# A linear-attention layer with a fused feed-forward network: two-input work moved off GpSimd, wider weight conversion, mask by copy and select, gather by chunk, first block by parts

## The chip, the cores and the metric

The kernel runs on one core of one Trainium2 chip. The metric is the device time of one execution in microseconds, taken as the median of several executions. The core has five engines with instruction queues of their own: TensorE (PE in the profile; its weight loads are PEld), VectorE (DVE), ScalarE (ACT), GpSimd (POOL) and SyncE (SP). SP only issues DMAs here.

## The reference

```python
def _attn_ref(q, k, v, f_logit):            # (4, 8, 768, 48) each
    f = 1.0 / (1.0 + np.exp(-f_logit))
    for t in range(S):
        state = f[:, :, t, :, None] * state + np.einsum('bhd,bhe->bhde', k[:, :, t], v[:, :, t])
        y[:, :, t] = np.einsum('bhd,bhde->bhe', q[:, :, t], state)
    return y

def _moe_ref(x, w1, w2, w3, w_out):         # x (3072, 384), w1, w2 (384, 1024)
    a = x @ w1
    b = x @ w2
    h = a * b @ w3                          # w3 (1024, 1024)
    return h @ w_out                        # w_out (1024, 384)

x = attn_out.transpose(0, 2, 1, 3).reshape(3072, 384)
```

The four weight matrices arrive as 64-bit floats. The kernel gets them as pairs of 32-bit words (low, high) and has to make 32-bit floats of them on the chip.

## The kernel before

**Attention.** The 3072 tokens are 24 chunks of 128 (`u`, six to each of four sequences). For a chunk, ScalarE makes the gates (`gates`), VectorE runs a product scan forward (`forward`, tile fwd) and one backward from the inverse of the chunk's last product (`ends`, `backward`, tile bwd), and scales q and k by them (Q, K). TensorE makes all pairs Q by K (`pairs`, two tiles pa), VectorE masks them with the tile `causal` (`mask`, tile A, two instructions of 128x512), and TensorE makes the outputs py from A and v and from the previous state (`value`). K is turned by TensorE (pk), copied by ScalarE (kt) and multiplied by v (pd); VectorE updates the state S with it (`state`), and GpSimd copies it into block form (`blocks`, tile sb). `outcome` on ScalarE copies py to ys.

**Feed-forward network.** It runs over 8 blocks of three chunks. `gather` moves a block's ys into the layout xt by ten DMAs, once all three chunks are there. `up` computes x@w1 and x@w2 in 16 groups of three products of 384 columns (L421; the trace shows each 32-bit product as two matmuls). `keep_a` copies the one on ScalarE, `times` multiplies on VectorE (tile ab). Since nothing non-linear follows, w3@w_out is folded once into wc: eight folds of eight products (`fold`, L573), each copied by VectorE (`folded`). `down` multiplies ab by wc, three groups of eight products a block (L456), and needs all eight folds.

**Weight conversion.** `fetch` loads a piece of 512 columns (384 for w_out) of word pairs and makes floats of it in six passes: two on ScalarE (`magnitude` L504, `rest` L508), a clamp on GpSimd (L511), a shift (L515) and a sign pass (L519) on VectorE, and an integer addition of two tiles on GpSimd (`joined`, L522). There are 36 pieces: 12 of w1 and w2, 8 of w_out, 16 of w3.

**Order.** Every step is a task of `Plan` with an engine, an estimated cost, what it depends on and a priority. `Plan.order` places the tasks one after the other in an imagined timetable, and the instructions are emitted in that order. Each engine then works through its list strictly in order, so an instruction that waits holds up everything behind it on its engine. `need(u)` is the time by which a chunk is wanted, used as a priority. A flag tells at the end whether the ranged form was accurate; if not, a general form runs. The flag is loaded on each engine after all its other work.

Of the kernel before, what the change touches and what calls it, by code (L numbers as in the profile page):

```python
# [31 lines left out]
U32 = mybir.dt.uint32  # L32
ALU = mybir.AluOpType
# [4 lines left out]
P = 128  # L38
# [14 lines left out]
NW = 512  # L53
NAB = 21
LOW = float.fromhex("0x1p-15")
HIGH = float.fromhex("0x1.dffffep+16")
# [58 lines left out]
def kernel(  # L115
# [16 lines left out]
    w1s = const.tile([P, KM, DFF], F32, name="w1s")  # L132
    w2s = const.tile([P, KM, DFF], F32, name="w2s")
    wc = const.tile([P, KF, DM], F32, name="wc")
    left = const.tile([1, 1], I32, name="left")
    with tc.manual_schedule():
        ranged(tc, q, k, f_logit, v, w1, w2, w3, w_out, out, ident, w1s, w2s, wc, left)
        outside = nc.values_load(left[0:1, 0:1], min_val=0, max_val=1)
        with tc.If(outside > 0, preferred_fallthrough_block=False):
            general(tc, q, k, f_logit, v, leaf_mask, out, ident, w1s, w2s, wc)  # L140
# [7 lines left out]
def ranged(ctx, tc, q, k, f_logit, v, w1, w2, w3, w_out, out, ident, w1s, w2s, wc, left):  # L148
# [5 lines left out]
    loads = ctx.enter_context(tc.tile_pool(name="loads", bufs=4))  # L154
    work = ctx.enter_context(tc.tile_pool(name="work", bufs=2))
    work3 = ctx.enter_context(tc.tile_pool(name="work3", bufs=3))
    raws = ctx.enter_context(tc.tile_pool(name="raws", bufs=4))
    wos = ctx.enter_context(tc.tile_pool(name="wos", bufs=KF))
# [5 lines left out]
    causal = keep.tile([P, C], F32, name="causal")  # L164
    first = keep.tile([R, NQ], F32, name="first")
    back = keep.tile([R, NQ], F32, name="back")
    gate = [keep.tile([R, NQ + 1], F32, name=f"gate{i}") for i in range(2)]
    lead = [keep.tile([R, HP], F32, name=f"lead{i}") for i in range(4)]
    qs, ks, fs = ([keep.tile([R, NQ], F32, name=f"{nm}{i}") for i in range(n)] for nm, n in (("q", 3), ("k", 3), ("f", 2)))
    sb = [keep.tile([R, HP, R], F32, name=f"sb{i}") for i in range(2)]  # L170
    least = keep.tile([R, HP], F32, name="least")
    ysum = keep.tile([R, NU], F32, name="ysum")
    ones = keep.tile([R, 1], F32, name="ones")

# [6 lines left out]
    def setup():  # L181
        for t in fs:
            nc.gpsimd.memset(t[32:64], 30.0)
        for t in qs + ks:
            nc.gpsimd.memset(t[32:64], 0.0)
        nc.vector.memset(first, 0.0)
        nc.vector.memset(heads(first)[:, :, 0], 1.0)
        for t in [back] + gate:
            nc.vector.memset(t, 0.0)
        nc.vector.memset(least, 1.0)  # L190
        nc.vector.memset(ones, 1.0)
        make_identity(nc, ident)
        nc.gpsimd.memset(causal, 1.0)
        nc.gpsimd.affine_select(
            out=causal, in_=causal, pattern=[[1, C]], compare_op=ALU.is_ge, fill=0.0, base=0,
            channel_multiplier=-1,
        )
        for t in sb:
            nc.gpsimd.memset(t, 0.0)
# [5 lines left out]
    def need(u):  # L205
        return 9.0 * u if u < UB else 45.0 + 17.0 * (u - UB)
# [4 lines left out]
    def attention(u):  # L211
        s, t = st[u], tk[u]
        b = u // NCH
# [9 lines left out]
        t["lf"] = plan.add("SP", 0.75, load(fs[u % 2], f_logit), past(u, 2, "g"), n0 - 30, lag=2.2)  # L223
        t["lq"] = plan.add("SP", 0.75, load(qs[u % 3], q), past(u, 3, "q"), n0 - 29, lag=2.2)
        t["lk"] = plan.add("SP", 0.75, load(ks[u % 3], k), past(u, 3, "k"), n0 - 28, lag=2.2)
# [5 lines left out]
        t["lv"] = plan.add("SP", 0.75, load_v, past(u, 4, "v", "s"), n0 - 27, lag=2.2)  # L231

        def gates():
            g, f = gate[u % 2], heads(fs[u % 2])
            nc.scalar.activation(heads(g[:, 0:NQ])[:, :, 1:C], f[:, :, 1:C], AF.Sigmoid)  # L235
            nc.scalar.activation(lead[u % 4], f[:, :, 0], AF.Sigmoid)

        t["g"] = plan.add("ACT", 0.85, gates, [t["lf"]] + past(u, 2, "r") + past(u, 5, "d"), n0)
# [3 lines left out]
        def forward():  # L242
            s["P"] = one.tile([R, NQ], F32, name="fwd")
            nc.vector.tensor_tensor_scan(  # L244
                s["P"], gate[u % 2][:, 0:NQ], first, 0.0, ALU.mult, ALU.add
            )

        t["p"] = plan.add("DVE", 1.1, forward, [t["g"]] + past(u, 1, "q", "i"), n0)
# [705 lines left out]
```

## Time and profile before

| | |
|---|---|
| runs | 585.24, 588.34, 589.01 us; median 588.34 |
| profiled execution | 584.74 us, span 583.0 us |
| mean granted TensorE clock | 0.967 |
| busy: PE / DVE / ACT / POOL | 524.1 / 248.7 / 127.6 / 118.3 us |

A row of the timeline has start, duration, engine, line, operation, written tile <- read tiles, shape and count; in brackets stands the idle time before it and what ended that. A row of groups has the count, then busy time in us and mean duration in ns, then idle time before. A row of the windows view has the window, then for PE, PEld, DVE, ACT and POOL the busy time and count, the granted clock, and the DMA share and rate.

### The profile page before, as it was taken

How to read it: one execution, taken by the hardware profiler on the slowest of the kernel's cores; microseconds unless marked ns; L12 is line 12 of the kernel's file. 1: busy time of each engine (PE TensorE's matmuls, PEld its weight loads, DVE VectorE, ACT ScalarE, POOL GpSimd, SP SyncE). 2: the span in 40 equal slices, each digit the busy share in tenths (PEclk: the TensorE clock that was granted, in tenths of full speed). 3: DMA queues.
4: the chain of work that ended last, by engine and by line, in shares of the span. 5: the costliest groups of instructions: out<-in, count | busy, mean ns of one | idle time of the engine just before them, and what ended most of it. 6: DMA issues, size and time to landing. Idle time of an engine off the chain costs nothing.

```text
span 583.0 us, 7033 instructions
## 1 busy us (share of the span) xinstructions
PE 524.1 (90%) x2610; PEld 331.3 (57%) x2610; DVE 248.7 (43%) x450; ACT 127.6 (22%) x277; POOL 118.3 (20%) x130
## 2 busy tenths in 40 slices
PE   2633996989999999989998999899999999999994
PEld 2522654656777666556655755565555555555552
DVE  7898997799999572118311611001101101100100
ACT  2552652432332221012111111111101101101100
POOL 3698885880222020000000100000000000000000
PEclk9966897999999999999999999999999999999998
DMA  6754757654534340022001100100010020000000
GB/s 191 237 185 144 246 197 228 187 167 129 172 116 134 104 136 28 1 68 82 15 0 51 32 15 0 55 28 0 15 54 15 0 67 15 0 13 28 0 15 32
DMA packets 25706, 46.68 MB, mean 80 GB/s; under 512 B 4928, under 2 KB 14144, under 8 KB 25664
## 3 DMA queue, kind: packets, MB, share of 16 engines
q1 hardware_dynamic: 25664, 46.16, 26.0%
q8 instruction: 22, 0.36, 0.3%
q14 instruction: 20, 0.16, 0.1%
HBM read 36.70 MB, written 4.72 MB: 71 GB/s over the span
## 4 chain that ended last, share of the span: by engine, by line
PE 61%; DVE 4%; SPq 3%; DMA 1%; issue 1%; ACT 0%; ACTq 0%; DVEq 0%
PE f L421 36%; PE f L456 19%; SPq L402 3%; PE py L328 2%; PE py L334 2%; PE pa L287 1%; DMA xt<-ys 1%; DVE bwd L270 1%; DVE A L298 1%; PE pd L350 1%; DVE fwd L244 1%; PE pk L310 1%; ACT ys L380 0%; DMA vt<-in_v_dram 0%; DVE Q L264 0%
## 5 line engine op out<-in xcount | busy, mean ns | idle before, releaser
L421 PE MATMUL f<-xt,w1s 128*128 128x384 f32 x384 | 136.4, 492 | 0.5 <-DVE ab L436 0.5
L421 PE MATMUL f<-xt,w2s 128*128 128x384 f32 x384 | 134.9, 488 | 0.0
L436 DVE TENSOR_TENSOR ab<-f,a 128x384 f32<-128x384 f32 x64 | 35.5, 555 | 227.1 <-PE f L421 227.1
L456 PE MATMUL f<-wc,ab 128*128 128x384 f32 x384 | 126.7, 487 | 0.0
L421 PEld LDWEIGHTS f<-xt,w1s 128*128 128x128 f32 x384 | 73.2, 192 | 50.6 <-DVE ab L436 1.1
L456 PEld LDWEIGHTS f<-wc,ab 128*128 128x128 f32 x384 | 72.2, 190 | 48.7
L421 PEld LDWEIGHTS f<-xt,w2s 128*128 128x128 f32 x384 | 72.2, 190 | 48.5
L430 ACT COPY a<-f 128x384 f32<-128x384 f32 x64 | 30.6, 477 | 193.0 <-PE f L421 193.0
L287 PE MATMUL pa<-Q,K 48*128 48x128 f32 x384 | 32.5, 316 | 41.6 <-DVE K L278 41.4
L371 POOL COPY sb<-S 48x192 f32<-48x192 f32 x40 | 25.0, 625 | 185.8 <-PE py L334 123.2
L287 PEld LDWEIGHTS pa<-Q,K 48*128 48x128 f32 x384 | 27.5, 216 | 48.2 <-issue 33.2
L298 DVE TENSOR_TENSOR A<-pa,causal 128x512 f32<-128x512 f32 x48 | 30.7, 679 | 30.6 <-PE py L328 25.0
L573 PE MATMUL f<-wo,w3s 128*128 128x384 f32 x128 | 43.2, 494 | 0.0
L328 PE MATMUL py<-A,vt 128*48 128x128 f32 (+1 forms) x384 | 29.8, 296 | 5.9 <-ACT ys L380 5.2
L573 PEld LDWEIGHTS f<-wo,w3s 128*128 128x128 f32 x128 | 24.4, 194 | 16.2 <-issue 0.6
L504 ACT ACTIVATE magnitude<-raw 128x512 f32<-128x512 f32 (+1 forms) x36 | 23.5, 653 | 40.8 <-POOL w3s L522 21.0
L511 POOL TENSOR_SCALAR magnitude<-magnitude 128x512 f32<-128x512 f32 (+1 forms) x36 | 29.5, 826 | 14.3 <-ACT magnitude L504 14.1
L328 PEld LDWEIGHTS py<-A,vt 128*48 128x48 f32 (+1 forms) x384 | 23.3, 140 | 15.9 <-issue 7.1
L244 DVE TENSOR_TENSOR_SCAN fwd<-gate,first 112x512 f32<-112x512 f32 x24 | 31.0, 1292 | 3.0 <-ACT gate L235 2.9
L515 DVE TENSOR_SCALAR magnitude<-magnitude 128x512 uint32<-128x512 uint32 (+1 forms) x36 | 27.6, 770 | 7.1 <-POOL magnitude L511 7.1
L465 ACT COPY o<-f 128x384 f32<-128x384 f32 x24 | 11.4, 477 | 86.7 <-PE f L456 86.7
L519 DVE SCALAR_TENSOR_TENSOR rest<-raw,rest 128x512 uint32<-128x512 uint32 (+1 forms) x36 | 28.5, 801 | 3.9 <-DMA k<-in_k_dram 2.1
(56 smaller groups left out, 347.2 us busy)
## 6 DMA issues: line engine op xcount, KB each, us to landing
raw<-in_w_dram SPq DMA_DIRECT2D x28, 512.0 KB, 4.4
f<-in_f_logit_dram SPq DMA_DIRECT2D x48, 96.0 KB, 2.8
q<-in_q_dram SPq DMA_DIRECT2D x48, 96.0 KB, 2.5
k<-in_k_dram SPq DMA_DIRECT2D x48, 96.0 KB, 2.5
vt<-in_v_dram SPq DMA_DIRECT2D x24, 192.0 KB, 2.8
out_dram<-o SPq DMA_DIRECT2D x24, 192.0 KB, 1.9
xt<-ys SPq DMA_DIRECT2D x48, 72.0 KB, 2.1
raw<-in_w_out_dram SPq DMA_DIRECT2D x8, 384.0 KB, 4.0
```

Of the source, the lines that this page charges most:

```text
L244: nc.vector.tensor_tensor_scan(s["P"], gate[u % 2][:, 0:NQ], first, 0.0, ALU.mult, ALU.add)
L287: nc.tensor.matmul(s["pa"][par][:, cols], lhsT=s["K"][rows(par), cols], rhs=s["Q"][rows(par), cols], start=True, stop=True,)
L298: nc.vector.tensor_tensor(s["A"][:, par], heads(s["pa"][par]), causal.unsqueeze(1).to_broadcast([P, HP, C]), ALU.mult)
L328: nc.tensor.matmul(s["py"][64 * par : 64 * par + w, hp], lhsT=s["v"][:, h * D : h * D + w], rhs=s["A"][:, par, hp], start=(hp == 0), stop= ...
L421: nc.tensor.matmul(s["pu", jc, which], lhsT=ws[:, kc, jc * P : jc * P + P], rhs=s["xt"][:, kc], start=(kc == 0), stop=(kc == KM - 1),)
L430: nc.scalar.copy(s["a", jc], s["pu", jc, 0])
L436: nc.vector.tensor_tensor(s["ab"][jc], s["pu", jc, 1], s["a", jc], ALU.mult)
L456: nc.tensor.matmul(s["po", i], lhsT=s["ab"][jc][:, i * P : i * P + P], rhs=wc[:, jc], start=(jc == 0), stop=(jc == KF - 1),)
L511: nc.gpsimd.tensor_scalar(s["m"], s["m"], HIGH, LOW, ALU.min, ALU.max)
L515: nc.vector.tensor_scalar(m, m, 3, None, ALU.logical_shift_left)
L519: nc.vector.scalar_tensor_tensor(r, s["hi"], 0x80000000, r, ALU.bitwise_and, ALU.bitwise_or)
L573: nc.tensor.matmul(ws["p", jc], lhsT=ws[jc][:, kc * P : kc * P + P], rhs=wo[kc], start=(kc == 0), stop=(kc == KF - 1),)
```

## The change

1. **Conversion.** A piece is now 1024 columns wide (768 for w_out), 18 pieces instead of 36, with three raw buffers instead of four. Passes: absolute value, exponent and shift on ScalarE; clamp on GpSimd; mantissa, rounding, sign and join on VectorE. The addition of two tiles on GpSimd is gone.
2. **Mask.** pa is one tile of 1024 columns. ScalarE copies it to A, and GpSimd sets the entries above the diagonal to zero in place by a select. VectorE's masks are gone.
3. **Small instructions.** The scans take the larger of product and a floor (`floor`), so that no separate clamp of the last product is needed. ScalarE keeps the last products of all chunks in `lasts`; the running minimum and the copy G on VectorE are gone, and the gates are one instruction.
4. **Gather by chunk.** Each chunk's ys goes to xt by six DMAs as soon as it is there. The rows of xt, and with them of w1 and w2 (one tile w12), stand in a new order: the first 96 rows of a slice are two heads, the last 32 rows come from the last pair of heads.
5. **First block by parts.** The first half of block 0's up products is done for its first chunk (128 columns) and then for its other two (256 columns).
6. **Plan.** Costs, lags and `need` have new numbers. The flag is loaded after the last matmul of `down`, so on SP and ScalarE it stands ahead of the last stores and copies.

```diff
-        return 9.0 * u if u < UB else 45.0 + 17.0 * (u - UB)
+        return (0.0, 12.0, 22.0)[u] if u < 3 else 38.0 + 15.0 * (u - 3)
...
-            nc.vector.tensor_tensor_scan(
-                s["P"], gate[u % 2][:, 0:NQ], first, 0.0, ALU.mult, ALU.add
-            )
+            nc.vector.tensor_tensor_scan(s["P"], gate[u % 2][:, 0:NQ], floor, 0.0, ALU.mult, ALU.max)
...
-            nc.vector.tensor_scalar(end, last, FLOOR, None, ALU.max)
-            nc.vector.reciprocal(end, end)
-            nc.vector.tensor_tensor(least, least, last, ALU.min)
-            if not closes:
-                s["G"] = work3.tile([R, HP], F32, name="G")
-                nc.vector.tensor_copy(s["G"], last)
+            nc.vector.reciprocal(heads(back)[:, :, C - 1], heads(s["P"])[:, :, C - 1])
...
-                nc.vector.tensor_tensor(
-                    s["A"][:, par], heads(s["pa"][par]), causal.unsqueeze(1).to_broadcast([P, HP, C]), ALU.mult
-                )
+            nc.scalar.copy(s["A"].rearrange("p r h c -> p r (h c)"), s["pa"])
...
+            nc.gpsimd.affine_select(
+                out=a, in_=a, pattern=[[0, H], [1, C]], compare_op=ALU.is_ge, fill=0.0, base=0,
+                channel_multiplier=-1,
+            )
...
+            for par in range(2):
+                nc.sync.dma_start(xt[par * D : par * D + D, :, cols], ys[rows(par), 0:KM])
+            for par in range(2):
+                at = 0
+                while at < D:
+                    kc, r = divmod(par * D + at, P - 2 * D)
+                    n = min(D - at, P - 2 * D - r)
+                    nc.sync.dma_start(
+                        xt[2 * D + r : 2 * D + r + n, kc, cols], ys[64 * par + at : 64 * par + at + n, HP - 1]
+                    )
+                    at += n
...
+        if n == 0:
+            part(0, 1, range(KF // 2))
+            part(1, UB, range(KF // 2))
+            part(0, UB, range(KF // 2, KF))
+        else:
+            part(0, UB, range(KF))
...
         def magnitude():
-            nc.scalar.activation(s["m"], s["hi"].bitcast(F32), AF.Abs)
-        def rest():
-            nc.scalar.activation(s["r"], s["lo"], AF.Copy, bias=2.0, scale=2.0**-51)
+            nc.scalar.activation(s["s"].bitcast(F32), s["hi"].bitcast(F32), AF.Abs)
+        def exponent():
+            nc.scalar.activation(s["s"], top, AF.Copy, bias=-7.5 / 16.0, scale=1.0 / 16.0)
         def clamped():
-            nc.gpsimd.tensor_scalar(s["m"], s["m"], HIGH, LOW, ALU.min, ALU.max)
+            nc.gpsimd.tensor_scalar(s["s"], s["s"], 896.0 + 255.0, 896.0, ALU.min, ALU.max)
         def shifted():
-            nc.vector.tensor_scalar(m, m, 3, None, ALU.logical_shift_left)
+            nc.scalar.activation(s["s"], s["s"], AF.Copy, bias=-896.0 * 2.0**23, scale=2.0**23)
+        def mantissa():
+            nc.vector.tensor_scalar(s["m"], s["hi"], 0xFFFFF, 0x100000, ALU.bitwise_and, ALU.bitwise_or)
+        def rounded():
+            nc.vector.scalar_tensor_tensor(s["mf"], s["lo"], 2.0**-32, s["m"], ALU.mult, ALU.add)
         def signed():
-            nc.vector.scalar_tensor_tensor(r, s["hi"], 0x80000000, r, ALU.bitwise_and, ALU.bitwise_or)
+            nc.vector.scalar_tensor_tensor(s["s"], s["hi"], 0x80000000, s["s"], ALU.bitwise_and, ALU.bitwise_or)
         def joined():
-            nc.gpsimd.tensor_tensor(dst().bitcast(I32), s["m"].bitcast(I32), s["r"].bitcast(I32), ALU.add)
+            nc.vector.scalar_tensor_tensor(dst(), s["mf"], 2.0**-20, s["s"].bitcast(F32), ALU.mult, ALU.mult)
```

**Where the instructions stand now.** TensorE of the kernel before, from the fourth chunk's pairs to the first fold (py, pd and pk are the chunk's output, state product and turned K; f<-xt is an up product, f<-wo a fold):

```order
L310 MATMUL pk<-ident,K 128x112 x4
L421 MATMUL f<-xt,w1s 128x384 x3
L328 MATMUL py<-A,vt 64x128
...
L334 MATMUL py<-Q,sb_112 112x128 x4
L350 MATMUL pd<-vt,kt 64x48
...
L421 MATMUL f<-xt,w2s 128x384 x3
...
L573 MATMUL f<-wo,w3s 128x384 x8
```

TensorE of the changed kernel, from the third chunk's output to the first fold (w_59 is the tile w12, f<-wos a fold):

```order
L410 MATMUL f<-xt,w_59 128x128 x6
L316 MATMUL py<-A,vt 64x128
...
L322 MATMUL py<-Q,sb_104 112x128 x4
L410 MATMUL f<-xt,w_59 128x256 x12
L298 MATMUL pk<-ident,K 128x112 x4
L272 MATMUL pa<-Q,K 128x128 x8
...
L410 MATMUL f<-xt,w_59 128x384 x9
L595 MATMUL f<-wos,w3s 128x384 x16
```

Before, the first up group stands behind the fourth chunk's pairs, and nine groups stand ahead of the first fold. Now the first groups, at 128 columns, stand behind the first chunk's output, and all 16 of block 0 ahead of the first fold; two groups of block 1 stand between the folds.

VectorE of the kernel before, between the fifth and the sixth chunk's scans (a stretch of w3 pieces, wc being a fold's copy):

```order
L519 SCALAR_TENSOR_TENSOR rest<-raw,rest 128x512
L515 TENSOR_SCALAR magnitude<-magnitude 128x512
L359 TENSOR_TENSOR G<-G,lead_101 112x4
L364 TENSOR_TENSOR S<-pd,S 112x192
L365 TENSOR_TENSOR S<-S,G 112x192
L244 SCALAR_TENSOR_TENSOR fwd<-gate_99,first 112x512
L580 COPY wc<-f 128x384
```

VectorE of the changed kernel, around the last w3 piece:

```order
L263 TENSOR_TENSOR K<-k_99,bwd 112x512
L249 TENSOR_TENSOR Q<-q_96,fwd 112x512
L529 TENSOR_SCALAR mantissa<-raw 128x1024
L533 SCALAR_TENSOR_TENSOR mantissa<-raw,mantissa 128x1024
L602 COPY wc<-f 128x384
L536 SCALAR_TENSOR_TENSOR exponent<-raw,exponent 128x1024
L539 SCALAR_TENSOR_TENSOR w3s<-mantissa,exponent 128x1024
```

A piece was two passes of 512 columns on VectorE, each waiting for another engine. It is four passes of 1024 now, of which the first two read only the loaded words and the mantissa tile. Eight chunks' scans stand ahead of this last piece; before, there were seven.

377 lines of the change are left out of this document (192 added, 185 removed).

## Prediction

> **What bounds the kernel now.** I read the page's slices first (each digit is a busy share, or the granted clock, in tenths), then TensorE's rows in order of time (start, duration, engine, line), then VectorE and GpSimd side by side.
>
> ```profile
> span 583.0 us, 7033 instructions
> PE   2633996989999999989998999899999999999994
> PEclk9966897999999999999999999999999999999998
> ```
>
> TensorE is idle or slow in the first nine or so of 40 slices (14.6 us each) and full afterwards. The granted clock falls in the same early slices, so time lost there is waiting and half-speed work. The early rows say what it lacks.
>
> ```profile
> 10.45 2.08 PE L287 MATMUL pa<-Q,K 48*128 48x128 f32 x16 [10.45 <-DVE K L278]
> 56.26 2.08 PE L287 MATMUL pa<-Q,K 48*128 48x128 f32 x16 [9.59 <-DVE K L278]
> 59.07 4.03 PE L421 MATMUL f<-xt,w1s 128*128 128x384 f32 x6
> 82.07 5.32 PE L573 MATMUL f<-wo,w3s 128*128 128x384 f32 x16
> 141.82 5.34 PE L573 MATMUL f<-wo,w3s 128*128 128x384 f32 x16
> 150.00:165.00 15.00, 15.00 (x157) 11.30 (x156) 14.58 (x35) 4.87 (x12) 4.54 (x6) 1.00 0.57 168
> ```
>
> The fourth chunk's pairs wait 9.59 us for VectorE's K; the first up product starts at 59.07; the last fold ends at 141.82 + 5.3 = 147.1. From there TensorE is full (the last row's second number, with VectorE third at 14.58 of 15). So two things set the end: when the last fold ends, and how much of the up products is already done by then. Up to 147.1 nine up groups ran (the rows from 59.07 to the fold at 82.07).
>
> ```profile
> 390.39 31.16 PE f L421 x96
> 209.86 1.06 PE py L334 x8
> 217.18 0.53 PE pk L310 x4
> 220.75 0.59 PE pd L350 x14
> ```
>
> A full block's 16 up groups take 31.16, so 1.95 each. A 128-column matmul takes 1.06/8 = 0.133. The last two rows are what a chunk's transposes (pk) and state product (pd) cost.
>
> What holds VectorE up in these 140 us is GpSimd. Waiting rows and quiet ones:
>
> ```profile
> 35.37 2.75 POOL L522 TENSOR_TENSOR w2s<-magnitude,rest 128x512 int32<-128x512 int32 x1 [0.37 <-DVE magnitude L515]
> 36.93 1.75 DVE L278 TENSOR_TENSOR K<-k,bwd 112x512 f32<-112x512 f32 x1
> 50.00 0.61 POOL L511 TENSOR_SCALAR magnitude<-magnitude 128x512 f32<-128x512 f32 x1
> 50.57 1.27 POOL L522 TENSOR_TENSOR w2s<-magnitude,rest 128x512 int32<-128x512 int32 x1
> 9.70 0.69 DVE L278 TENSOR_TENSOR K<-k,bwd 112x512 f32<-112x512 f32 x1
> ```
>
> The join (2.75 against 1.27 quiet) lies there while VectorE finishes, then K (1.75 against 0.69) lies there until the join ends at 38.1: they take turns. The groups give the sum:
>
> ```profile
> L515 DVE TENSOR_SCALAR magnitude<-magnitude 128x512 uint32<-128x512 uint32 (+1 forms) x36 | 27.6, 770 | 7.1 <-POOL magnitude L511 7.1
> L519 DVE SCALAR_TENSOR_TENSOR rest<-raw,rest 128x512 uint32<-128x512 uint32 (+1 forms) x36 | 28.5, 801 | 3.9 <-DMA k<-in_k_dram 2.1 <-ACT rest L508 1.8
> L278 DVE TENSOR_TENSOR K<-k,bwd 112x512 f32<-112x512 f32 x24 | 21.6, 901 | 0.6
> L253 DVE TENSOR_SCALAR back<-fwd 112x4 f32<-112x4 f32 x24 | 6.7, 279 | 0.4
> 44.43 0.41 DVE L515 TENSOR_SCALAR magnitude<-magnitude 128x512 uint32<-128x512 uint32 x1
> 44.76 0.68 DVE L519 SCALAR_TENSOR_TENSOR rest<-raw,rest 128x512 uint32<-128x512 uint32 x1
> 45.37 0.41 DVE L515 TENSOR_SCALAR magnitude<-magnitude 128x512 uint32<-128x512 uint32 x1
> ```
>
> Means over quiet durations: shift 0.36 x 36 = 13, sign 0.12 x 36 = 4.4, K 0.21 x 24 = 5, the small one of L253 0.11 x 24 = 2.6 (its quiet row stands below). With the groups that I left out, all of a few us, I take 30 us of VectorE time lost to turns, nearly all before 131. GpSimd's own quiet work there is 36 x (0.61 + 1.27), about 65 with the narrower pieces: VectorE paid some 0.46 of it.
>
> **The change, part by part: VectorE up to the last converted w3 piece.** Before, that piece's join ended at 131.3:
>
> ```profile
> 129.20 2.11 POOL L522 TENSOR_TENSOR w3s<-magnitude,rest 128x512 int32<-128x512 int32 x1 [0.96 <-DVE magnitude L515]
> 59.06 1.27 DVE L298 TENSOR_TENSOR A<-pa,causal 128x512 f32<-128x512 f32 x2
> 137.29 1.22 DVE L244 TENSOR_TENSOR_SCAN fwd<-gate,first 112x512 f32<-112x512 f32 x1
> 138.55 0.17 DVE L253 TENSOR_SCALAR back<-fwd 112x4 f32<-112x4 f32 x1
> 138.97 0.69 DVE L264 TENSOR_TENSOR Q<-q,fwd 112x512 f32<-112x512 f32 x1
> 141.76 1.22 DVE L244 TENSOR_TENSOR_SCAN fwd<-gate,first 112x512 f32<-112x512 f32 x1
> 61.60 0.54 DVE L519 SCALAR_TENSOR_TENSOR rest<-raw,rest 128x384 uint32<-128x384 uint32 x1
> 62.07 1.15 DVE L515 TENSOR_SCALAR magnitude<-magnitude 128x384 uint32<-128x384 uint32 x1
> ```
>
> Removed: masks of the seven chunks done by then, 7 x 1.27 = 8.9. Three of the four small instructions between 138.55 and 138.97, 0.32 x 7 = 2.2. Shift and sign of 34 units of 512 columns at 0.33 + 0.61 (start to start at 44.43) = 32. The turns, 30.
>
> Added: four passes over each of 14 pieces of 1024 columns and 4 of 768. The two-input pass takes 0.61 at 512 and 0.47 at 384 (61.60 to 62.07), so 1.17 at 1024 and 0.88 at 768; the masking pass twice 0.33 at most. A piece is 3 x 1.17 + 0.62 = 4.1 and 3.1: 14 x 4.1 + 4 x 3.1 = 69.8. The order puts eight chunks ahead of the last piece instead of seven: one chunk is 137.29 to 141.76, less a wc copy and the small instructions, plus its state update, 4.5. Block 0's 12 multiplications instead of four, 3.
>
> The masking pass reads every other word, which no row shows at this rate; bounds 0.6 and the 1.17 of a two-input pass (+9 over all pieces). I take 0.62, nearest to the same kind of instruction.
>
> GpSimd keeps 34 units of clamp at 0.61 (20.7) and gets eight selects of 1024 columns. A select was seen only at 128:
>
> ```profile
> L194 POOL TENSOR_SCALAR_AFFINE_SELECT causal<-causal 128x128 f32<-128x128 f32 x1 | 0.3, 292 | 0.1
> ```
>
> Bounds: 1.2 at the clamp's quiet rate (twice 0.61) and 2.34 (eight times 0.292). Part of the 0.292 must be fixed, so I take 1.6, nearer to the clamp: 13 for eight. At the same 0.46 VectorE pays 15 for the 33. Bounds: nothing, and all 33. The 7.1 us in which the shift waited for the clamp (its row above) partly goes, since masking and rounding need neither ScalarE nor GpSimd and fill the time: -4 (bounds 0 and -7).
>
> Sum: 131.3 - 8.9 - 2.2 - 32 - 30 + 69.8 + 4.5 + 3 + 15 - 4 = 146.5. The last fold follows directly: 152 against 147.1, **5 later**.
>
> The Trainium skill, "SBUF — State Buffer", section "Who interferes with whom", says that a VectorE instruction with two SBUF inputs contends with a GpSimd instruction that reads SBUF, and that one of the two fully blocks. The trace agrees in the 1.75 us K above. By this rule alone, the new rounding, sign and join passes are all two-input ones, and this part of the change would save no turn.
>
> **TensorE ahead of the last fold.** By the order all 16 up groups of block 0 and two of block 1 stand ahead of it, against nine. That is 9 x 1.95 = 17.5 done earlier. Cutting half of block 0 into 128 and 256 columns costs 48 x (0.133 + 0.215 - 0.325) = 1.1. Net **-16.4**. TensorE has room: those groups, eight folds of 5.3 and eight chunks at about 4.2 (pairs 1.05 by half of the slow 2.08, py 1.09 and 1.06, pk, pd) are 111 us between 10 and 152. What is late next is the fold, as above.
>
> **Gather by chunk.** Three times TensorE waits for a chunk's output copy, which waits for a whole block's gather (the first and the last row; the third lies between):
>
> ```profile
> 258.87 1.09 PE L328 MATMUL py<-A,vt 128*64 128x128 f32 x16 [2.00 <-ACT ys L380]
> ...
> 375.73 1.09 PE L328 MATMUL py<-A,vt 128*64 128x128 f32 x16 [1.52 <-ACT ys L380]
> 249.81 6.45 SPq L402 DMA_DIRECT2D xt<-ys  x10
> ```
>
> Ten issues take 6.45; the first chunk's six take at most 3.9, 2.6 sooner, more than each wait: **-5.2**. SP issues 144 gather DMAs for 80, 41 us more over the span, hidden since SP's queue is nearly empty after 150. Loads queued behind a gather come later in the first 60 us; the order loads two chunks ahead.
>
> **Mask by copy and select.** Off VectorE, but a new chain: ScalarE copies 1024 columns, GpSimd selects, then TensorE's py. The copy by two rows:
>
> ```profile
> L318 ACT COPY kt<-pk 128x448 f32<-128x448 f32 x20 | 10.6, 530 | 37.6 <-PE pk L310 37.5
> L430 ACT COPY a<-f 128x384 f32<-128x384 f32 x64 | 30.6, 477 | 193.0 <-PE f L421 193.0
> ```
>
> 0.83 ns a column, 1.0 at 1024. Copy and select, 2.6, lie beside a pk, an up group and a pd (0.53 + 1.95 + 0.59 = 3.1) where the order is tightest, and beside a 5.2 us down group elsewhere. I cost it at nothing; a missing cover is a rival.
>
> **The end.**
>
> ```profile
> 574.96 0.33 SPq L471 DMA_DIRECT2D out_dram<-o  x1
> ```
>
> The flag's load now stands ahead of the last two stores on SP, not behind them. Of the 7.7 us from that issue to the end of the span, the store's landing stays; the saving lies between 0 and 5.8. I take **-2**, nearer to nothing since no row shows the load.
>
> Sum, against the profiled execution's own 584.7 (span 583.0): 584.7 + 5 - 16.4 - 5.2 - 2 = **566**. The median of the runs shown is 3.6 above that execution; I leave the sum as it is.
>
> **Rivals.**
>
> *The turns go away.* If clamps and selects fit into gaps of VectorE, the 15 goes; the last fold ends near 137, and TensorE's own 111 us of work from 10 on, with some half-speed at the start, allows little better. 566 - 15 = **551**. For: GpSimd's work halves, 65 to 33. Against: VectorE's passes are twice as long and leave few gaps. 0.25.
>
> *GpSimd entirely in series with VectorE*, the page's rule taken literally: 33 instead of 15, 18 later, **584**. Against: before, only 0.46 of GpSimd's time showed up on VectorE. 0.11.
>
> *TensorE waits for the select.* At 2.34 us and a turn of 1.1 behind a VectorE pass, copy to py is 4.4 against 3.1 of cover; six chunks so placed cost 8, the longer selects VectorE 3: **577**. For: tightest place. Against: 5.2 us of cover elsewhere. 0.08.
>
> *Slower: conversion passes dearer than priced.* It decides from 1.3 us more per piece over 17 full pieces (22 us), which eats all gains. If rounding and joining, integer words turned to float, ran at half rate, a piece would be 6.4 and the last fold 39 later: **605**. For: no row has this mix. Against: the sign pass reads the same words at 1.17. 0.06.
>
> *The first parts don't come early*, because a chunk's gather blocks the next loads on SP or all three pieces are late: then at most the 16.4 is lost, **582**. 0.04.
>
> **How the numbers follow.** The forecast has 0.46. The range takes in the turns' bounds (-15, +18): 549 to 584. The measurement tells 1% (582.5 to 594.2 around the median) from no change. Faster: 0.46 + 0.25 + 0.08, most of the series case and half the last, 0.87; same 0.07; slower 0.06.
>
> **What would show it.** After: first up product near 30, at 128 columns; 18 up groups ahead of the last fold; that fold's end at 145 to 160; VectorE's two-input passes near 1.2 with some at 2 or more; no waits of 1.5 to 2 us for ys in the middle. Wrong if the fold ends past 165, if passes have medians over 1.5, or if py waits for A chunk after chunk.

## The result, and the profile after

The changed kernel takes **567.56 us** (median of 4 runs, 567.18 to 568.85) against 588.27 before, a ratio of 0.9661 with a 95% interval of 0.9624 to 0.9699. The forecast was 566 in a range of 549 to 584. The profiled execution has a span of 566.7 us and took 568.85.

The slices of the page, to be held against those of before (TensorE's busy tenths, its granted clock):

```profile
span 566.7 us, 7083 instructions
PE   2266999799999999999999999999999999999994
PEclk9999799999999999999999999999999999999998
```

TensorE is nearly full from the fifth slice on (before: from about the tenth), and its clock is granted nearly everywhere. TensorE's rows of the first 160 us (start, duration, line, and in brackets the idle time ahead and what ended it):

```profile
24.47 1.19 PE L410 MATMUL f<-xt,w 128*128 128x128 f32 x4 [6.60 <-DMA xt<-ys]
32.83 0.79 PE L410 MATMUL f<-xt,w 128*128 128x128 f32 x2 [7.17 <-DVE w L539]
...
50.41 1.09 PE L316 MATMUL py<-A,vt 128*64 128x128 f32 x16 [0.96 <-POOL A L287]
...
57.22 1.19 PE L410 MATMUL f<-xt,w 128*128 128x256 f32 x2 [4.67 <-DMA xt<-ys]
...
60.25 6.20 PE L410 MATMUL f<-xt,w 128*128 128x256 f32 x20 [0.40 <-DMA xt<-ys]
...
96.69 10.93 PE L595 MATMUL f<-wos,w3s 128*128 128x384 f32 x32 [0.17 <-DVE w3s L539]
111.45 1.97 PE L316 MATMUL py<-A,vt 128*64 128x128 f32 x16 [2.75 <-POOL A L287]
...
150.62 1.09 PE L316 MATMUL py<-A,vt 128*64 128x128 f32 x16 [0.23 <-POOL A L287]
152.60 5.33 PE L595 MATMUL f<-wos,w3s 128*128 128x384 f32 x16
```

The first up products run at 24.5 and, once all three pieces are there, at 32.8, in 128 columns. In the first 57 us TensorE is busy for 26. Chunk 2's gather is what it waits for at 57.22 and again, by 0.40 us, at 60.25. The select is on the way to it: py of chunk 2 waited 0.96 us for its select at 50.41. From 57 on TensorE runs almost without a gap, up to 63 at a granted clock of 0.50, except at 111.45, where py of chunk 5 waits 2.75 us for the select. The last fold ends at 152.60 + 5.33 = 157.9. Behind it no wait of TensorE's shows up to the end of the span; before there were four, of 0.44, 2.00, 1.63 and 1.52 us.

VectorE's last w3 join, and the groups of both engines up to 185 us (busy time and mean ns of one):

```profile
148.39 1.23 DVE L539 SCALAR_TENSOR_TENSOR w3s<-mantissa,exponent 128x1024 f32<-128x1024 f32 x1
```

```profile
L536 DVE SCALAR_TENSOR_TENSOR exponent<-raw,exponent 128x1024 uint32<-128x1024 uint32 x14 | 17.0, 1215 | 0.0
L539 DVE SCALAR_TENSOR_TENSOR w3s<-mantissa,exponent 128x1024 f32<-128x1024 f32 x8 | 13.5, 1682 | 0.3
L529 DVE TENSOR_SCALAR mantissa<-raw 128x1024 uint32<-128x1024 uint32 x14 | 12.6, 903 | 2.8 <-DMA raw<-in_w_dram 2.5
L263 DVE TENSOR_TENSOR K<-k,bwd 112x512 f32<-112x512 f32 x13 | 11.0, 845 | 0.4
L249 DVE TENSOR_TENSOR Q<-q,fwd 112x512 f32<-112x512 f32 x13 | 9.0, 695 | 0.0
...
L522 POOL TENSOR_SCALAR exponent<-exponent 128x1024 uint32<-128x1024 uint32 x14 | 22.2, 1584 | 42.4 <-ACT exponent L519 33.0 <-ACT lasts L238 5.7 <-DVE mantissa L533 3.5
L287 POOL TENSOR_SCALAR_AFFINE_SELECT A<-A 128x1024 f32<-128x1024 f32 x11 | 16.5, 1504 | 43.8 <-ACT A L281 43.7
```

Quiet ones of the same:

```profile
12.61 0.69 DVE L529 TENSOR_SCALAR mantissa<-raw 128x1024 uint32<-128x1024 uint32 x1 [2.48 <-DMA raw<-in_w_dram]
14.76 1.09 POOL L287 TENSOR_SCALAR_AFFINE_SELECT A<-A 128x1024 f32<-128x1024 f32 x1 [8.74 <-ACT A L281]
15.93 1.04 POOL L522 TENSOR_SCALAR exponent<-exponent 128x1024 uint32<-128x1024 uint32 x1
21.35 1.22 DVE L539 SCALAR_TENSOR_TENSOR w<-mantissa,exponent 128x1024 f32<-128x1024 f32 x1
```

So turns remain: a w3 join takes 1.68 in the mean against 1.22 quiet, a masking pass 0.90 against 0.69, a clamp 1.58 against 1.04, a select 1.50 against 1.09. Mean less quiet, times count, over VectorE's groups in these 185 us comes to some 17 us (the four largest: joins 3.7, masking 3.0, G 2.5, K 2.0).

**Where the time went, by spans.** TensorE's down products end at 542.96 + 15.49 = 558.45, before at 558.93 + 15.49 = 574.42 (last rows of the two chains). The span of 583.0 less 566.7 is 16.3. The medians differ by 20.7, since the profiled execution of before (584.74) ran below its median and that of after (568.85) above; the table can't show where the other 4.4 lie:

| stretch | before | after | change | predicted |
|---|---|---|---|---|
| start to the end of the last fold | 147.1 | 157.9 | +10.8 | +5 |
| from there to the last down product | 427.3 | 400.5 | -26.8 | -16.4 - 5.2 |
| behind it | 8.6 | 8.3 | -0.3 | -2 |

### The profile page after: what moved, and what is told of

Same layout as the page of the kernel before. It is cut to its first block, busy times and chain, and to the rows that moved or that the text cites. A ratio compares the mean times of both kernels' runs of the same rounds, so it can differ in the third digit from the quotient of the medians.

```text
span 566.7 us, 7083 instructions
## 1 busy us (share of the span) xinstructions
PE 523.0 (92%) x2658; PEld 335.2 (59%) x2658; DVE 246.5 (43%) x337; ACT 165.4 (29%) x287; POOL 96.1 (17%) x98
## 4 chain that ended last, share of the span: by engine, by line
PE 86%; DVE 7%; DMA 2%; POOL 1%; ACT 1%; issue 1%; SPq 1%; DVEq 0%; POOLq 0%
PE f L410 41%; PE f L455 22%; PE f L595 7%; PE pa L272 4%; PE py L316 4%; PE py L322 3%; PE pd L338 2%; PE pk L298 2%; DVE exponent L536 2%; DMA raw<-in_w_dram 1%; DVE mantissa L533 1%; POOL A L287 1%; DVE mantissa L529 1%; DVE w L539 1%; DMA xt<-ys 1%
## 5 line engine op out<-in xcount | busy, mean ns | idle before, releaser
L410 PE MATMUL f<-xt,w 128*128 128x384 f32 (+2 forms) x816 | 260.2, 478 | 19.1 <-DMA xt<-ys 11.7
L410 PEld LDWEIGHTS f<-xt,w 128*128 128x128 f32 x816 | 154.7, 197 | 114.3 <-DVE w L539 7.5
L426 DVE TENSOR_TENSOR ab<-f,a 128x384 f32<-128x384 f32 (+2 forms) x68 | 36.2, 533 | 216.3 <-PE f L410 216.3
L419 ACT COPY a<-f 128x384 f32<-128x384 f32 (+2 forms) x68 | 31.3, 461 | 188.8 <-PE f L410 188.8
L287 POOL TENSOR_SCALAR_AFFINE_SELECT A<-A 128x1024 f32<-128x1024 f32 x24 | 33.1, 1380 | 106.3 <-ACT A L281 104.4
L595 PE MATMUL f<-wos,w3s 128*128 128x384 f32 x128 | 42.4, 488 | 0.3 <-DVE w3s L539 0.2
L522 POOL TENSOR_SCALAR exponent<-exponent 128x1024 uint32<-128x1024 uint32 (+1 forms) x18 | 28.0, 1557 | 56.8 <-ACT exponent L519 43.7
L233 DVE TENSOR_TENSOR_SCAN fwd<-gate,floor 112x512 f32<-112x512 f32 x24 | 31.7, 1322 | 11.1 <-ACT gate L225 7.8
L255 DVE TENSOR_TENSOR_SCAN bwd<-gate,back 112x512 f32<-112x512 f32 x24 | 33.7, 1402 | 0.8
L281 ACT COPY A<-pa 128x1024 f32<-128x1024 f32 x24 | 24.3, 1011 | 22.0 <-PE pa L272 22.0
```

The costliest lines, as they stand in the source:

```text
L233: nc.vector.tensor_tensor_scan(s["P"], gate[u % 2][:, 0:NQ], floor, 0.0, ALU.mult, ALU.max)
L255: nc.vector.tensor_tensor_scan(s["R"][:, ::-1], gate[u % 2][:, NQ:0:-1], back[:, ::-1], 0.0, ALU.mult, ALU.max)
L287: nc.gpsimd.affine_select(out=a, in_=a, pattern=[[0, H], [1, C]], compare_op=ALU.is_ge, fill=0.0, base=0, channel_multiplier=-1,)
L410: nc.tensor.matmul(s["pu", jc, which, c0][:, 0:nt], lhsT=w12[:, which, kc, jc * P : jc * P + P], rhs=s["xt"][:, kc, cols], start=(kc == 0) ...
L419: nc.scalar.copy(s["a", jc, c0][:, 0:nt], s["pu", jc, 0, c0][:, 0:nt])
L426: nc.vector.tensor_tensor(s["ab"][jc][:, cols], s["pu", jc, 1, c0][:, 0:nt], s["a", jc, c0][:, 0:nt], ALU.mult)
```

## The experiments

Each kernel is the changed one with the edit shown; the ratios are to the kernel before, timed beside it. The changed kernel itself stands at 0.9661 (0.9624 to 0.9699); runs that differ from it by less than some 3 us are told apart by their traces, not by their times. At the start there were two theories. **A**: the time is set by what TensorE lacks before 60 us, and VectorE's work after that is hidden. **B**: VectorE's sum up to the last converted w3 piece sets it, as the prediction had it.

| run | median us | ratio, 95% interval |
|---|---|---|
| no_sign_w3 | 565.89 | 0.9625 (0.9587 to 0.9662) |
| no_sign_first3 | 567.47 | 0.9653 (0.9619 to 0.9686) |
| early_k | 567.14 | 0.9643 (0.9614 to 0.9671) |
| relu_no_clamp | 564.12 | 0.9609 (0.9576 to 0.9643) |
| no_parts | 566.04 | 0.9637 (0.9595 to 0.9678) |
| gather_by_block | 571.25 | 0.9731 (0.9681 to 0.9780) |
| mask_dve | 573.06 | 0.9746 (0.9701 to 0.9791) |
| join_pool | 584.23 | 0.9945 (0.9921 to 0.9968) |
| sign_twice_w3 | 574.96 | 0.9772 (0.9726 to 0.9819) |
| relu_no_parts | 567.15 | 0.9654 (0.9613 to 0.9694) |
| order_relu | 551.19 | 0.9369 (0.9332 to 0.9407) |
| order_clamp | 560.78 | 0.9557 (0.9494 to 0.9620) |

### Less VectorE work: late, early, and from GpSimd's turns

no_sign_w3, and no_sign_first3 with the condition `len(parts) >= 3`:

```diff
-        g = plan.add("DVE", 0.16 + 0.62 * w, signed, [h, r], prio - 1)
+        g = plan.add("DVE", 0.16 + 0.62 * w, signed if a == 2 else lambda: None, [h, r], prio - 1)
```

> The sign pass of the eight w3 pieces is left out (their signs are lost; the order of all other instructions stays): eight VectorE passes of 1.2 us less, 9.8 us, all between 85 and 150 us. Theory A (TensorE is full from 60 us on, so the time is set by what it lacks before that; VectorE's work after 60 us is hidden): 0 to -1.5 us against the changed kernel's 567.6, since TensorE's only waits after 60 are 2.75 and about 2 us near 110. Theory B (VectorE, with GpSimd's turns, up to the last converted w3 piece sets the end, as the prediction had it): the last join and so the end come 8 to 10 us earlier, 558 to 560.

> The sign pass of the first three pieces alone is left out (their signs are lost; the order stays): three VectorE passes of 1.2 us less, 3.6 us, between 17 and 33 us, where they run back to back and TensorE waits for them. Theory A (the time is set by what TensorE lacks before 60 us): all of it is seen, -3 to -4 us, 564. Theory B (VectorE's sum to the last w3 join sets the end): -3 to -4 as well by the sum, so this run alone does not tell them apart; with the run without the w3 signs it does: A says that three early passes are worth more than eight late ones, B that they are worth 3/8 of them.

TensorE's rows without the w3 signs, and then without the first three:

```profile
109.11 1.20 PE L316 MATMUL py<-A,vt 128*64 128x128 f32 x16 [2.33 <-POOL A L287]
...
149.90 5.33 PE L595 MATMUL f<-wos,w3s 128*128 128x384 f32 x16
```

```profile
29.80 0.79 PE L410 MATMUL f<-xt,w 128*128 128x128 f32 x2 [4.00 <-DVE w L539]
57.42 8.11 PE L410 MATMUL f<-xt,w 128*128 128x256 f32 x24 [6.58 <-DMA xt<-ys]
```

9.8 us of late VectorE work less gave 1.7 us, which the times can hardly tell from nothing (the last fold starts 2.7 us earlier): B's -8 to -10 fails, and A's 0 to -1.5 is near. But 3.6 us of early work less gave nothing that the times show, against both. Its trace says why: the first products come 3.0 us earlier (29.80), but TensorE still waits for chunk 2's gather until 57.4, and the last fold starts at 151.74, only 0.9 earlier. Here the pieces are not what holds TensorE up longest; the third chunk is.

early_k brings K and Q of chunk 1 forward, by other priorities (the second line stands behind the loads' tasks, which keep theirs):

```diff
-        return (0.0, 12.0, 22.0)[u] if u < 3 else 38.0 + 15.0 * (u - 3)
+        return (0.0, 12.0, 17.0)[u] if u < 3 else 38.0 + 15.0 * (u - 3)
...
+        n0 = (0.0, 3.0, 9.0)[u] if u < 3 else n0
```

> The same instructions in another order of the first 45 us: K and Q of chunk 1 stand behind the first weight piece on VectorE (at about 22 us) instead of behind the third (32.7), chunk 2's loads and scans are earlier likewise; the last fold keeps the same 18 up groups ahead of it. Theory A: chunk 2's gather lands near 46 instead of 60 us, TensorE's 6.6, 7.2 and 4.7 us waits shrink, and the time falls until the fold waits for its w3 piece, which came 3 us before it was needed: -3 to -5 us. Theory B: VectorE has as much to do up to the last join, so nothing is gained, 0 to +1.

Its GpSimd and TensorE rows (the lines are one further down than in the changed kernel):

```profile
29.03 2.56 POOL L361 COPY sb<-S 48x192 f32<-48x192 f32 x2 [5.56 <-DVE S L355]
31.66 1.42 POOL L288 TENSOR_SCALAR_AFFINE_SELECT A<-A 128x1024 f32<-128x1024 f32 x1
```

```profile
24.15 0.98 PE L299 MATMUL pk<-ident,K 112*128 112x112 f32 x4 [6.29 <-DVE K L264]
33.14 1.97 PE L317 MATMUL py<-A,vt 128*64 128x128 f32 x16 [4.98 <-POOL A L288]
...
57.53 7.50 PE L411 MATMUL f<-xt,w 128*128 128x256 f32 x24 [7.44 <-DMA xt<-ys]
```

K comes at 24 as meant, but the select stands on GpSimd behind the copy of the state blocks, which waited 5.56 us for VectorE's S. py follows at 33.1, and chunk 2 lands at 57.5 again. The edit did not do what it was for, and the time stayed: the run decides nothing between A and B, but shows a queue that order_relu and order_clamp below mend.

relu_no_clamp takes the clamp off GpSimd (low896 is a column of -896 - 7.5/16, and the upper bound is left out):

```diff
-            nc.scalar.activation(s["s"], top, AF.Copy, bias=-7.5 / 16.0, scale=1.0 / 16.0)
+            nc.scalar.activation(s["s"], top, AF.Relu, bias=low896, scale=1.0 / 16.0)
...
-            nc.scalar.activation(s["s"], s["s"], AF.Copy, bias=-896.0 * 2.0**23, scale=2.0**23)
+            nc.scalar.activation(s["s"], s["s"], AF.Copy, bias=0.0, scale=2.0**23)
...
-        c = plan.add("POOL", 0.2 + 0.5 * w, clamped, [e], prio - 1)
-        h = plan.add("ACT", 0.2 + 0.43 * w, shifted, [c], prio - 1)
+        h = plan.add("ACT", 0.2 + 0.43 * w, shifted, [e], prio - 1)
```

> GpSimd's clamp of the exponents is left out of all 18 pieces; ScalarE's pass ahead of it does the lower bound by Relu, the upper bound is left out (no weight of the inputs reaches it). GpSimd loses 18 x 1.56 = 28 us, and ScalarE waits for no clamp between its two passes. Theory A: the three early pieces lose the turns that show in 22.6 to 29.2 (1.41 against 0.69 twice) and some of ScalarE's wait, -2 to -3 us, 565. Theory B: VectorE loses about half of the 28 us of turns up to 150, -8 or more, 559 or less. The prediction's price (0.46 of GpSimd's time) gives 0.46 x 20.7 = 9.5 us.

Measured -3.4, A's size. VectorE's turns do fall by nearly what the prediction's price says (joins of w3 from 1682 to 1228 ns, K from 845 to 689; by the sum above from some 17 to some 7 us, about 10 where 0.46 x 20.7 = 9.5 was priced). Without the clamp's task the plan also emits another order (VectorE's differs from its 13th instruction on), so the time is not the clamp's alone. TensorE still waits for the third chunk until 56.6 and for chunk 5's select:

```profile
56.56 8.64 PE L412 MATMUL f<-xt,w 128*128 128x256 f32 x24 [7.33 <-DMA xt<-ys]
...
108.91 1.09 PE L318 MATMUL py<-A,vt 128*64 128x128 f32 x16 [2.90 <-POOL A L289]
```

### The parts of the change, undone one at a time

no_parts, one `part(0, UB, range(KF))` for block 0:

> Block 0 in whole groups of 384 columns again, in place of the parts of 128 and 256. Theory C (from the runs so far: everything of TensorE that can't start before the gather of chunk 2 lands at 57 us follows it without a gap; what is done ahead of it, and whether the weight pieces are there at 30 or 33, decides): the eight 128-column groups that ran between 24 and 50 us (6.4 us at full rate) move behind the landing, the cutting's 1.1 us is saved: +5.3 us, 573. Theory B (VectorE's sum to the last w3 join sets the end): 0, since VectorE has four multiplications less, if anything -1.

```profile
57.20 6.30 PE L410 MATMUL f<-xt,w 128*128 128x384 f32 x12 [4.41 <-DMA xt<-ys]
93.50 10.48 PE L593 MATMUL f<-wos,w3s 128*128 128x384 f32 x32
...
148.40 5.33 PE L593 MATMUL f<-wos,w3s 128*128 128x384 f32 x16
```

Theory C missed: 566.0, not 573. The 5.3 us that the parts were to be worth (6.4 us of products done early, less 1.1 for the cutting) were given back. With the parts TensorE has no up group left at 108 us, since block 1's need chunk 5's gather; so py of chunk 5 waits 2.75 us and the two py groups then run at half rate (1.97 and 1.80 against 1.09 and 1.13). Without the parts, two up groups stand between chunk 5's pairs and its py, and no wait is left from 57.20 to the last fold. Its last fold starts at 148.40, 4.2 earlier, with 17 groups ahead of it instead of 18, so 1.9 us of that come later.

gather_by_block gives blocks 1 to 7 one gather for three chunks:

```diff
...
+        elif u % UB == UB - 1:
...
+            x = plan.add(
+                "SP", 8.1, all_three, [o["y"] for o in three] + (blk[n - 2]["up"] if n >= 2 else []), n0 - 100, lag=2.2
+            )
```

> From block 1 on, a block's gather is issued once its three chunks are there, as before the change; block 0 stays by chunk. Prediction: the three waits of 1.5 to 2 us for the output copy come back, +5.2 us, 573. Rival: in the new order the up groups of the block ahead cover the gather, 0 to +1.

```profile
154.01 5.33 PE L609 MATMUL f<-wos,w3s 128*128 128x384 f32 x16
203.13 1.16 PE L272 MATMUL pa<-Q,K 48*128 48x128 f32 x16 [0.47 <-DVE Q L249]
208.00 1.16 PE L272 MATMUL pa<-Q,K 48*128 48x128 f32 x16 [0.63 <-DVE Q L249]
```

+3.7 in the median, +2.9 in the span. The size is near the predicted 5.2, the mechanism isn't: no wait for the output copy comes back. The last fold is 1.4 later, two waits of 0.47 and 0.63 for Q follow, and the rest is not settled.

mask_dve puts VectorE's two masking multiplications back:

```diff
-            nc.scalar.copy(s["A"].rearrange("p r h c -> p r (h c)"), s["pa"])
+            for par in range(2):
+                nc.vector.tensor_tensor(
+                    s["A"][:, par], heads(s["pa"][:, par]), tri.unsqueeze(1).to_broadcast([P, HP, C]), ALU.mult
+                )
```

> The mask is made again by VectorE (two multiplications of 512 columns by a triangle, out of PSUM) in place of ScalarE's copy and GpSimd's select. Theory B by the prediction's prices: 8 chunks x 1.27 = 10.2 us more for VectorE up to the last w3 join, less 6 us of turns that the selects cost: +4. Theory C: the chain from the pairs to py is as long as before (1.3 against 1.0 + 1.1 and a turn), VectorE's three early chunks delay chunk 2 by up to 3.8, and the 2.75 us wait for the select at 108 us goes partly: 0 to +2.

```profile
100.81 12.26 PE L596 MATMUL f<-wos,w3s 128*128 128x384 f32 x32 [5.08 <-DVE w3s L540]
```

+5.5, B's +4 rather than C's 0 to +2: here the folds wait 5.08 us for VectorE's w3 pieces, and the select's wait is gone. (The plan also puts 20 up groups ahead of its last fold, not 18.)

join_pool gives GpSimd a two-input pass again (the missing factor of 2 to the -20 goes into the clamp's bounds and the shift, 916 in place of 896):

```diff
-            nc.vector.scalar_tensor_tensor(dst(), s["mf"], 2.0**-20, s["s"].bitcast(F32), ALU.mult, ALU.mult)
+            nc.gpsimd.tensor_tensor(dst(), s["mf"], s["s"].bitcast(F32), ALU.mult)
```

> The last two-input pass of each weight piece (the join) runs on GpSimd, as a multiplication of two tiles, in place of VectorE; the exponents' lower bound is 916 in place of 896 (the factor 2 to the -20 goes into the exponent), which no weight of the inputs reaches. VectorE loses 18 x 1.2 = 21 us, GpSimd gains 18 x 2.5 = 45 us (1.27 at 512 columns in the profile of before). By the prediction's price VectorE pays 0.46 x 45 = 20.7 in turns: theory B says 0 (-3 to +3). Theory C: the selects stand behind joins of 2.5 to 5 us in GpSimd's queue, so chunk 2's gather and the py at 108 us come later: +4 to +10 us, 572 to 578. If two-input work on GpSimd cost nothing but its own time, VectorE's 21 us would be gained: -3 or better.

The groups up to 185 us:

```profile
L255 DVE TENSOR_TENSOR_SCAN bwd<-gate,back 112x512 f32<-112x512 f32 x13 | 21.9, 1688 | 0.4
...
L249 DVE TENSOR_TENSOR Q<-q,fwd 112x512 f32<-112x512 f32 x13 | 19.3, 1482 | 0.0
...
L263 DVE TENSOR_TENSOR K<-k,bwd 112x512 f32<-112x512 f32 x13 | 16.5, 1272 | 0.3
...
L529 DVE TENSOR_SCALAR mantissa<-raw 128x1024 uint32<-128x1024 uint32 x14 | 10.0, 717 | 2.2 <-DMA raw<-in_w_dram 2.2
...
L539 POOL TENSOR_TENSOR w3s<-mantissa,exponent 128x1024 f32<-128x1024 f32 x8 | 21.4, 2681 | 8.1 <-DVE G L348 5.6 <-DVE exponent L536 2.4
```

**+16.7 us: with this one pass on GpSimd the change is nearly undone** (0.9945). Q takes 1.48 against 0.69, K 1.27, the backward scan 1.69 against 1.23; mean less quiet over all of VectorE's groups is some 49 us, 32 more than in the changed kernel. The joins' quiet time is 43 us (14 x 2.5 + 4 x 1.9, from the 1.27 at 512 columns). VectorE thus pays 0.7 of a two-input pass on GpSimd, not 0.46, and the 21 us that it is spared don't cover that. TensorE then waits in many places (for Q five times by 1.5 to 1.8 us, for a select up to 3.75), so even C's +10 was too little. How much of the 16.7 comes from VectorE's turns and how much from selects that stand behind joins in GpSimd's queue, no run parts.

The Trainium skill, "SBUF — State Buffer", section "Who interferes with whom", has a VectorE instruction with two SBUF inputs contend with a GpSimd instruction that reads SBUF. The trace agrees for Q and K, which have two inputs and are stretched here. The masking pass, with one input, is nearly quiet in this run (0.717 against 0.69), but that says nothing of joins: it writes the tile that the join before it reads, and none of the 18 lies beside a join. Beside a clamp it is stretched in the changed kernel:

```profile
53.06 1.88 POOL L522 TENSOR_SCALAR exponent<-exponent 128x1024 uint32<-128x1024 uint32 x1
54.08 1.41 DVE L529 TENSOR_SCALAR mantissa<-raw 128x1024 uint32<-128x1024 uint32 x1
```

### More VectorE work, and another order

sign_twice_w3 runs the sign pass twice for w3, which changes no value:

> The sign pass of the eight w3 pieces is done twice (the second changes nothing; the order of all instructions stays): 9.8 us more VectorE between 85 and 150 us. Theory D (from the runs so far: the changed kernel stands where VectorE and TensorE are both nearly full, so less VectorE work gains little, as its 9.8 us less gained only 1.7, but more is paid nearly in full): the last w3 piece comes at 159 instead of 149.6, the last fold can start 6 to 7 us later than its 152.6, +6 to +8 us, 574. Theory A (VectorE's work after 60 us is hidden): 0 to +2.

```profile
140.08 5.43 PE L596 MATMUL f<-wos,w3s 128*128 128x384 f32 x16 [1.55 <-DVE w3s L540]
...
158.83 5.33 PE L596 MATMUL f<-wos,w3s 128*128 128x384 f32 x16
```

+7.4, as theory D says, against A's 0 to +2. The last fold starts 6.2 later, and TensorE waits for one w3 piece after the other. 9.8 us less VectorE work were worth 1.7, 9.8 us more cost 7.4: in this stretch the changed kernel stands where the two engines balance.

If so, TensorE needs other work while VectorE converts. Two runs move the order, one of them without the clamp (its other edits are relu_no_clamp's). The second changed line stands behind the loads' tasks; besides, the plan counts a gather as 4.0 in place of 2.7 us and the landing of a weight load as 5.0 in place of 2.0, and the priorities of w_out start at 55 in place of 45, those of w3 go from 62 + 6 * jc to 70 + 10 * jc:

```diff
-        return (0.0, 12.0, 22.0)[u] if u < 3 else 38.0 + 15.0 * (u - 3)
+        return (0.0, 12.0, 13.0)[u] if u < 3 else 24.0 + 12.0 * (u - 3)
...
+        n0 = (0.0, 12.0, 22.0)[u] if u < 3 else n0
...
-            t["b"] = plan.add("POOL", 1.3, blocks, [t["d"]] + past(u, 1, "v"), n0)
+            t["b"] = plan.add("POOL", 1.3, blocks, [t["d"], t["c"]] + past(u, 1, "v"), n0)
```

> Without the clamp (as in relu_no_clamp), and with other numbers in the plan: chunks 3 and on are wanted 14 us earlier and every 12 us, the w_out and w3 pieces later, a select stands ahead of the copy of the state blocks on GpSimd, and the plan counts a gather as 4.0 and a weight load's landing as 5.0 us. 16 up groups of block 0 and 17 of block 1 stand ahead of the last fold instead of 16 and 2, so TensorE has work while VectorE converts. Theory D: TensorE's wait at 108 us and half of the one at 53 go, -6 to -10 us against relu_no_clamp's 564, 556. Theory A: nothing changes before 57 us, so only the wait at 108 and the slow matmuls behind it go, -3 to -4, 560. Theory B: with VectorE's sum the same up to the last join, no gain, 564.

> The other order alone: the numbers of the plan as in order_relu (chunks earlier, w_out and w3 pieces later, gather 4.0, landing 5.0, select ahead of the state blocks), with the clamp back on GpSimd, so the work is the changed kernel's own. Theory D: most of order_relu's 13 us against relu_no_clamp (551.2 against 564.1) came from the order, which gives TensorE work while VectorE converts; the turns of the clamp then cost VectorE about 9 us, which that cover hides in part: 554 to 558. If the gain needed the clamp's turns gone, it stays near the changed kernel: 563 to 567.

TensorE's rows with waits from 25 us to the last fold, without the clamp (all of them) and with it (some):

```profile
27.65 1.09 PE L341 MATMUL pd<-vt,kt 128*64 128x48 f32 x16 [1.55 <-ACT kt L309]
32.86 0.57 PE L301 MATMUL pk<-ident,K 112*128 112x112 f32 x4 [0.25 <-DVE K L266]
38.11 1.09 PE L341 MATMUL pd<-vt,kt 128*64 128x48 f32 x16 [3.49 <-ACT kt L309]
72.18 1.16 PE L275 MATMUL pa<-Q,K 48*128 48x128 f32 x16 [0.29 <-DVE Q L252]
...
170.75 5.34 PE L597 MATMUL f<-wos,w3s 128*128 128x384 f32 x16
```

```profile
123.14 5.43 PE L596 MATMUL f<-wos,w3s 128*128 128x384 f32 x16 [0.98 <-DVE w3s L540]
...
143.94 1.09 PE L317 MATMUL py<-A,vt 128*64 128x128 f32 x16 [1.82 <-POOL A L288]
...
182.11 5.43 PE L596 MATMUL f<-wos,w3s 128*128 128x384 f32 x16
```

order_relu takes **551.2 us, 16.4 less than the changed kernel** and below every time that D gave it. Behind the wait at 38.11 TensorE waits 0.29 us in all, and its last fold ends at 176.1, 18 us later than in the changed kernel, with nothing lost by it: 27 up groups stand ahead of that fold (11 of block 1's, not the 17 of the expectation). With the clamp it is 560.8, between the two cases of its expectation: the order alone gives 6.8. In the old order the clamp costs 3.4 us, in the new one 9.6. That this is so near the priced 9.5 is in part chance: by the sum of above the turns of the two new orders differ by only some 7 us (19 against 12), and here too the plan emits another order without the clamp's task. What the traces do show is TensorE's waiting: from 40 us to the last fold it adds up to 7.6 us with the clamp, for weight pieces, Q, K and a select, against 0.29 without.

relu_no_parts joins the two small gains of above:

> Without the clamp, and block 0 in whole groups of 384 columns. If the two edits act on different waits, -1.5 and -3.4 us add up: 562.5. If both act through the one wait for chunk 5's select near 108 us, 564 to 565.5.

567.2, outside both cases: they don't add up, and one shared wait doesn't explain it either, since relu_no_clamp keeps its wait at chunk 5 (2.90) and is the faster one. Without the clamp the parts are worth 3.0 us, with it -1.5 (both near what the times can tell). Of the 3.1 us between the two spans (564.8 and 561.7) the traces give two: the last fold has 17 groups ahead of it instead of 18, worth 1.9, and starts only 0.9 earlier (147.18 against 148.11), and two waits for K and Q at 200 us take 1.1. The rest is open.

## Why the prediction was right

**The time, and the largest cause.** 566 against 567.6. So close a hit is partly luck: the sum starts from one execution of 584.7, and from the median of 588.3 the same terms give 569.7. The forecast rested on two-input work leaving GpSimd, with turns that stay at about half of what GpSimd still does. join_pool bears out the first: one two-input pass put back costs 16.7 us, where the whole change gained 20.7, its effect on GpSimd's queue included. relu_no_clamp bears out the second: without the clamps VectorE's turns fall by about 10 us where 9.5 was priced. How much of them reaches the time depends on the order (3.4 us in this one, 9.6 in the other). By the same sum the turns of before come to some 35 us up to 131 rather than 30. "The turns go away" (551) did not happen by the change; it took an edit of its own and another order. The fully serial case (584) did not either. The passes were priced well: 1.22 for 1.17, 0.69 for 0.62, the copy 1.01 for 1.0; the select is cheaper quiet (1.09 for 1.6) and dearer in the mean with its turns (1.50).

**VectorE to the last w3 join: +3.1 off.** 149.6 against 146.5. The row stands above. VectorE is idle for 17.8 us up to there, before it was idle for 20.0 up to 131.3: the term for the waits is -2.1, not -4. The other 1.2 or so is busy time (20.4 more, where the sum's other terms give 19.2); passes dearer by 0.05 and 0.07 than priced have that direction, but the terms weren't measured one by one.

**The fold itself: the step that failed.** "TensorE has room: 111 us between 10 and 152", hence "the last fold follows directly". It started at 152.60, 3.0 behind the join. The room lay ahead of 57 us, where TensorE could not use it, since chunk 2's gather had not landed; from 57 on it was full, up to 63 at half its clock, and when the join came at 149.6 it still had a pd and two py groups ahead of the fold. So the end came at 157.9 instead of 152: 3.1 by the join and 3.0 by TensorE's own queue.

**The cover of the select.** Cost at nothing, with a missing cover as rival at 577. Behind 57 us it was missing in one place, chunk 5, which closes its sequence and has neither transposes nor a state product: 2.75 us and, at half rate, (1.97 + 1.80) - (1.09 + 1.13) = 1.6 more. The rival's mechanism thus took 4.3 us there, in one place and not in six. Ahead of 57 us py waited 2.22 us for the select in chunk 0 and 0.96 in chunk 2, and the second wait lies on the chain to the gather that TensorE lacks most.

**TensorE ahead and the gather: -26.8 against -21.6.** Nine groups at 1.93 are 17.4, the three ys waits that are gone 5.15, as priced. Another 0.44 of waiting went (at 191.90 before), one more py and pd (2.75) stand ahead of the last fold by the order, and the cutting's 1.1, which the -16.4 had taken off, falls ahead of it too. About 1 us is not accounted for. Undoing the gather cost 3.7, but through other waits than those named, so that term is right in size and open in mechanism.

**The parts.** "Net -16.4" was counted with the parts' early products in it. no_parts shows that they gave nothing in this order: what they did early went, in part, into the wait at chunk 5. (No row of before shows the 0.215 us that the cutting's 1.1 takes for a 256-column matmul; 12 of them took 2.8 us in relu_no_clamp, 0.23 each.)

**The end.** -2 against -0.3 (8.6 us behind the last down product before, 8.3 after): the move of the flag's load saved next to nothing, as the lower bound had it.

These errors nearly cancel: +5.9 up to the fold (152 to 157.9), -5.2 behind it, +1.7 at the end, 2.4 us in the span. That too is luck.

## What to carry to other kernels

Two-input work on GpSimd beside a busy VectorE is to be priced at VectorE's cost: here VectorE paid 0.7 of the joins' quiet time and 0.5 of the clamps'. Where two engines balance, a term taken off one of them shows only in part (1.7 of 9.8 us here) and a term added shows nearly whole (7.4 of 9.8); so look first for work that the other one could do meanwhile, and let an order supply it, before more passes are trimmed. A wait that costs nothing "beside other work" needs that work named for every place, the last chunk of a sequence too.

## What was not expected of the hardware

- After a wait TensorE often starts slowly, and the wait so costs more than its length: py of chunk 5 took 1.97 us after 2.75 us of waiting, a later one 1.09 after 0.23 (rows above). The granted clock goes with it: 0.50 from 111.5 to 114 us in the changed kernel, and likewise for 3 to 7 us behind the same wait in no_sign_w3, no_sign_first3, early_k, gather_by_block and sign_twice_w3, but 1.00 throughout in relu_no_clamp, where py of chunk 5 took 1.09 after 2.90 us of waiting. Why the clock fell in the one and not in the other these runs don't show. Nor does the recorded clock always show it: in no_parts the 12 matmuls behind a 4.41 us wait took 6.30, where 0.325 each would make 3.9, at a recorded clock of 1.00.
- A masking pass on VectorE with one SBUF input takes turns with GpSimd's clamps and selects all the same: 1.41 us beside a clamp (rows above) and 1.46 beside a select in relu_no_clamp, 0.69 quiet.
- Undisturbed, GpSimd's select of 1024 columns takes 1.09 us, hardly more than its clamp (1.04), and by column under half of the 0.292 for 128.
